# FFN of two batches at a time by seven block products, in a pooled-attention and mixture-of-depths kernel

## The chip, the cores and the metric

The kernel runs on one core of a Trainium2 chip. The metric is the device time of one execution in microseconds (us). The core has five engines that run their own instruction queues side by side: TensorE (PE in the profile, with its weight loads as PEld) for matrix products, VectorE (DVE), ScalarE (ACT), GpSimd (POOL), and SyncE (SP), which here starts the transfers between main memory and the on-chip memory (SBUF). Matrix products land in PSUM, from where ACT or DVE copy them. [...] a buffer that is used again makes its next writer wait for its last reader.

## The reference

Two stages follow each other. The first is attention with 8 batches, 8 heads, 1152 keys, 64 values per head, and queries averaged in pairs (576 rows). The second routes the 128 rows of each batch with the highest gate score through a feed-forward network (FFN) and adds the result, weighted by the gate, to those rows. All is float32.

```python
q_pool = q.reshape(B, H, S // 2, 2, D).mean(axis=3)
scores = np.matmul(q_pool, k.transpose(0, 1, 3, 2)) / np.sqrt(D)
attn = softmax(scores)                      # sum + 1e-9 in the divisor
x = np.matmul(attn, v)                      # -> (B, 576, 512), heads side by side

scores = x @ w_gate                         # (B, 576)
out = x.copy()
for b in range(B):
    top = argpartition(-scores[b], 128)[:128]
    xe = x[b, top]                          # 128 x 512
    ye = np.maximum(xe @ w1, 0) @ w2        # w1 512 x 1024, w2 1024 x 512
    g = 1 / (1 + np.exp(-scores[b, top]))
    out[b, top] = x[b, top] + g[:, None] * ye
```

## The kernel before

Two heads make a pair; 8 batches of 4 pairs are 32 pairs, and each is worked off in two halves of 288 query rows: 64 halves, numbered h. In half h, PE forms the scores of h (L818), ACT takes their exponentials into a tile p of which there are two (L825), POOL and DVE sum them, and PE forms the products of half h - 1 with v (L836). So p is used one half after it is made.

```python
def scores(self, half):
    ...
    p = half["p"] = self.work.tile([P, self.NG, G, 2, n], F32, name="p")     # work: 2 buffers
    for c in range(self.NC):                                                 # 9 blocks of keys
        sc = self.banks()                                                    # PSUM: 4 tiles of 2 banks
        for e in range(2):
            for j in range(2):
                nc.tensor.matmul(sc[keys, j, 0:n], lhsT=pair["kT"][...], rhs=pair["qT"][rows, qs], ...)  # L818
        nc.scalar.activation(p[:, c // G, c % G, :, :], sc[:, :, 0:n], AF.Exp, scale=self.scale)          # L825

def folded(self, half):                     # sums of the exponentials
    ...
    for u in range(G):
        nc.gpsimd.tensor_tensor(out=acc[:, u, :], in0=units[:, 0, u, :], in1=units[:, 1, u, :], op=ALU.add)  # L857
    for a, of in enumerate((units[:, 2, :, :], acc[:, :, :])):
        nc.vector.tensor_reduce(fold[:, a, :], of.rearrange(...), AX.X, ALU.add, apply_transpose=True)       # L862
    ...

def normalized(self, pair):
    ...
    rec = pair["rec"] = self.small.tile([P, self.QB], F32, name="rec")
    nc.vector.reciprocal(rec[:, :], tot)                                     # L954
    x = self.work.tile([P, self.QB, BLK], F32, name="x")
    nc.gpsimd.tensor_tensor(out=x, in0=pair["avb"], in1=rec (broadcast), op=ALU.mult)   # L956, shortened

def gated(self, half):
    ...
    nc.vector.tensor_reduce(pair["red"][:, ns], pair["prod"][:, ns, :], AX.X, ALU.add)
    if half["s"] == 1:
        nc.vector.tensor_tensor(out=pair["part"][:, pair["hp"], :], in0=pair["red"], in1=pair["rec"], op=ALU.mult)  # L981
        ...                                                                  # after 4 pairs: the batch is routed
```

Routing a batch is a generator (`routed`) whose pieces are laid between the pieces of the attention of later batches. It ranks the scores on DVE, finds the chosen rows (`index`, POOL, L1175), gathers them by an indirect transfer (`xe`), transposes them on PE (L1197), and then runs the FFN of that one batch:

```python
hT = ffn.tile([P, self.NFC, P], F32, name="hT")
for f0 in range(0, self.NFC, 4):                    # 8 blocks of 128 hidden units
    pv = self.banks()[:, 0, :].rearrange("p (c n) -> p c n", n=P)
    for f in range(4):
        for c in range(self.ND):                    # 4 blocks of 128 inputs
            nc.tensor.matmul(pv[:, f, 0:w], lhsT=self.w1[:, c, ...], rhs=xeT[:, c, 0:w], ...)   # L1208
        if f == 3:
            nc.scalar.activation(hT[:, f0 : f0 + 4, 0:w], pv[:, :, 0:w], AF.Relu)               # L1216
ps = self.banks()[:, 0, :]
for f in range(self.NFC):
    nc.tensor.matmul(ps[0:w, 0 : self.Dm], lhsT=hT[:, f, 0:w], rhs=self.w2[:, f, :], ...)       # L1221
...
nc.scalar.activation(y[0:w, :], ps[0:w, 0 : self.Dm], AF.Copy, scale=own_gate[0:w, 0:1])        # L1240
nc.gpsimd.tensor_tensor(out=xe[0:w, :], in0=y[0:w, :], in1=xe[0:w, :], op=ALU.add)              # L1245
nc.gpsimd.indirect_dma_start(out=rows_out, ..., in_=xe[0:w, :], ...)                            # L1246
```

Keys and queries (kb, qb) and values (v_sb) of a pair are loaded ahead: in the second half of pair n, those of pair n + 2. kb and qb have two buffers each, v_sb three. After the last half there is a tail: layer 2 of batch 5, the FFN of batch 6, and the routing and FFN of batch 7.

Of the kernel before, what the change touches and what calls it, by code (L numbers as in the profile page):

```python
# [10 lines left out]
P = 128  # L11
BLK = 32

G = 3
# [520 lines left out]
class _Plain:  # L535
# [10 lines left out]
    def __init__(self, ctx, tc, q, k, v, moe_w_gate, moe_w1, moe_w2, capacity, out):  # L546
# [27 lines left out]
        assert 0 < self.TAIL < P and self.Dm == self.ND * P and self.Dm <= 512  # L574
        assert self.F == self.NFC * P and self.NFC % 4 == 0
# [17 lines left out]
        self.w2 = self.const.tile([P, self.NFC, self.Dm], F32, name="w2")  # L593

# [21 lines left out]
    def constants(self):  # L616
# [13 lines left out]
        slot_i = self.ffn.tile([P, self.Sp], I32, name="cmp", bufs=1)  # L630
        nc.gpsimd.iota(slot_i[:, :], pattern=[[1, self.Sp]], base=0, channel_multiplier=0)
        self.slot_f = const.tile([P, self.Sp], F32, name="slot_f")
        nc.vector.tensor_copy(self.slot_f[:, :], slot_i[:, :])
# [34 lines left out]
    def line_of_scores(self):  # L668

        line = self.ffn.tile([P, self.NT * P], F32, name="sc_row")  # L670
        self.nc.gpsimd.memset(line[0:1, self.Sp :], 0.0)
        return line
# [24 lines left out]

    def load_pair(self, b, hp):  # L700
# [3 lines left out]
        qb = self.load.tile([P, self.QB, 2, BLK], F32, name="qb")  # L704
# [8 lines left out]
    def load_values(self, pair):  # L713


        nc, hp = self.nc, pair["hp"]
        v_sb = pair["v"] = self.load.tile([P, 2, self.NC, self.D], F32, name="v_sb", bufs=3)
        of = self.v[pair["b"], 2 * hp : 2 * hp + 2]
        of = of.rearrange("j (i g c) d -> g i j c d", i=BLK, c=self.NC)
        for g in range(P // BLK):  # L720
            nc.sync.dma_start(
                v_sb[g * BLK : (g + 1) * BLK, :, :, :].rearrange("i j c d -> i j (c d)"),
                of[g].rearrange("i j c d -> i j (c d)"),
            )
# [16 lines left out]
    def load_first(self, b, hp):  # L741
# [3 lines left out]
        kb = self.load.tile([P, self.KB, BLK], F32, name="kb")  # L745
        kn = kb.rearrange("p n d -> p (n d)").rearrange("p (c j d) -> p c j d", c=NC, j=2)
        acc = self.work.tile([P, G, 2 * self.HALF], F32, name="acc")
        third = self.QB // 3
        qn = acc.rearrange("p u n -> p (u n)")[0 : 3 * BLK, 0 : 4 * third * D]
        qn = qn.rearrange("p (j m d) -> p j m d", j=2, d=D)  # L750
        v_sb = self.load.tile([P, 2, NC, D], F32, name="v_sb", bufs=3)
# [11 lines left out]
        return {"k": kn, "q": qn, "v": v_sb, "b": b, "hp": hp}  # L763

    def prepare_first(self, pair):
# [5 lines left out]
        acc = self.work.tile([P, G, 2 * self.HALF], F32, name="acc")  # L771
        qp = acc.rearrange("p u n -> p (u n)")[0:rows, 0 : 2 * third * D]
        qp = qp.rearrange("p (n j d) -> p n j d", j=2, d=D)
# [76 lines left out]
    def folded(self, half):  # L850
# [9 lines left out]
        fold = self.small.tile([P, 2, G * nb], F32, name="fold")  # L860
# [8 lines left out]
        if half["s"] == 0:  # L869
            pair["sum"] = self.small.tile([P, 2, self.QB], F32, name="sum")  # L870
# [11 lines left out]
    def side_by_side(self, of):  # L882

        n = of.shape[-1]
        to = self.small.tile([BLK, P // BLK, n], F32, name="groups")
# [4 lines left out]
    def added(self, groups):  # L890
        n = groups.shape[-1]
        total = self.small.tile([BLK, n], F32, name="total")
# [26 lines left out]
    def multiplied(self, half):  # L919

        pair, hb, hp = half["pair"], self.HB, half["pair"]["hp"]
        if half["s"] == 0:
            pair["prod"] = self.work.tile([P, self.QB, BLK], F32, name="prod")
# [8 lines left out]
    def normalized(self, pair):  # L932
# [3 lines left out]
        if self.last_pair(pair):  # L936
# [16 lines left out]
        rec = pair["rec"] = self.small.tile([P, self.QB], F32, name="rec")  # L953
        nc.vector.reciprocal(rec[:, :], tot)  # L954
        x = self.work.tile([P, self.QB, BLK], F32, name="x")
        nc.gpsimd.tensor_tensor(  # L956
            out=x[:, :, :],
            in0=pair["avb"][:, :, :],
            in1=rec[:, :].unsqueeze(2).broadcast_to([P, self.QB, BLK]),
            op=ALU.mult,  # L960
        )
        pair["x"] = x
# [10 lines left out]
    def gated(self, half):  # L973

        nc, pair, hb = self.nc, half["pair"], self.HB
        if half["s"] == 0:
            pair["red"] = self.small.tile([P, self.QB], F32, name="red")
        ns = slice(half["s"] * hb, (half["s"] + 1) * hb)
        nc.vector.tensor_reduce(pair["red"][:, ns], pair["prod"][:, ns, :], AX.X, ALU.add)
        if half["s"] == 1:  # L980
            nc.vector.tensor_tensor(  # L981
# [5 lines left out]
            if pair["hp"] == self.NPAIR - 1:  # L987
                unit = self.routed(pair["b"], pair["part"])
                at = next(unit) == "mid"
                self.routing.append([pair["b"], unit, at])  # L990
# [6 lines left out]
    def routed(self, b, part):  # L997
# [8 lines left out]
        line = self.small.tile([P, self.QB], F32, name="line")  # L1006
# [4 lines left out]
        if b < self.B - 1:  # L1011
# [6 lines left out]
            else:  # L1018
                total = self.small.tile([BLK, self.QB], F32, name="total")
# [9 lines left out]
            sc_row = ffn.tile([P, NT * P], F32, name="sc_row")  # L1029
# [11 lines left out]
        else:  # L1041

            diag = ffn.tile([P, self.QB, BLK], F32, name="diag", bufs=1)
# [34 lines left out]
        for t, rows in tiles:  # L1078
            at = t * P
            cmp = ffn.tile([P, Sp], F32, name="cmp", bufs=1)  # L1080
# [20 lines left out]
            tie = ffn.tile([P, P], F32, name="tie", bufs=1)  # L1101
# [35 lines left out]
        for s0, w in self.slots:  # L1137
            pick = ffn.tile([P, NT, P], F32, name="pick", bufs=1)
            index = ffn.tile([P, 1], I32, name="index")
            own_gate = ffn.tile([P, 1], F32, name="own_gate")  # L1140
            if b == self.B - 1:
# [3 lines left out]
                    in0=self.slot_f[:, s0 : s0 + w].unsqueeze(1).broadcast_to([P, NT, w]),  # L1145
# [15 lines left out]
            else:  # L1161
# [13 lines left out]
                nc.gpsimd.tensor_scalar(  # L1175
# [6 lines left out]
            xe = ffn.tile([P, self.Dm], F32, name="xe")  # L1182
# [9 lines left out]
            yield mid  # L1192
# [8 lines left out]
            yield mid  # L1201

            hT = ffn.tile([P, self.NFC, P], F32, name="hT")
            for f0 in range(0, self.NFC, 4):
                pv = self.banks()[:, 0, :].rearrange("p (c n) -> p c n", n=P)
                for f in range(4):
                    for c in range(self.ND):
                        nc.tensor.matmul(  # L1208
                            pv[:, f, 0:w],
                            lhsT=self.w1[:, c, (f0 + f) * P : (f0 + f + 1) * P],  # L1210
                            rhs=xeT[:, c, 0:w],
                            start=(c == 0),
                            stop=(c == self.ND - 1),
                        )
                    if f == 3:
                        nc.scalar.activation(hT[:, f0 : f0 + 4, 0:w], pv[:, :, 0:w], AF.Relu)  # L1216
                    yield "hidden" if f0 + f == self.NFC - 1 else False

            ps = self.banks()[:, 0, :]
            for f in range(self.NFC):  # L1220
                nc.tensor.matmul(  # L1221
                    ps[0:w, 0 : self.Dm],
                    lhsT=hT[:, f, 0:w],
                    rhs=self.w2[:, f, :],
                    start=(f == 0),
                    stop=(f == self.NFC - 1),
                )
                yield False
            if b == self.B - 1:
                nc.vector.scalar_tensor_tensor(  # L1230
                    out=xe[0:w, :],
                    in0=ps[0:w, 0 : self.Dm],
                    scalar=own_gate[0:w, 0:1],
                    in1=xe[0:w, :],
                    op0=ALU.mult,
                    op1=ALU.add,
                )
            else:
                y = ffn.tile([P, self.Dm], F32, name="y", bufs=1)
                nc.scalar.activation(  # L1240
                    y[0:w, :], ps[0:w, 0 : self.Dm], AF.Copy, scale=own_gate[0:w, 0:1]
                )
                if b < self.B - 2:
                    yield True
# [227 lines left out]
```

## Time and profile before

Three runs: median 707.77 us (707.0 to 708.58). One profiled execution, span 704.8 us:

| engine | busy, us | share of the span |
|---|---|---|
| PE (products) | 694.4 | 99% |
| PEld (weight loads, beside PE) | 516.8 | 73% |
| DVE | 496.5 | 70% |
| POOL | 485.1 | 69% |
| ACT | 444.5 | 63% |

The 16 transfer engines moved 82.86 MB; the packets of the main queue took 58.1% of their time.

In a line of the groups, the name left of the arrow is what is written, the ones right of it what is read; then shape, type and count; after the first bar the busy time of all in us and the mean duration of one in ns; after the second bar the idle time of the engine ahead of them and who ended it. In a line of the chain the first number is the start in us, the second the length. A float32 matmul of the program shows as two records. Records of PE overlap, so a mean duration is longer than the pace at which they follow each other.

### The profile page before, as it was taken

The page shows a single profiled execution, that of the slowest core. Times are in us where ns is not written, and L with a number is a line of the kernel's source. Part 1 is how long each engine was busy: PE and PEld are TensorE (multiplying, and loading weights), DVE is VectorE, ACT ScalarE, POOL GpSimd, SP SyncE. Part 2 cuts the span into 40 slices and gives each one's busy share as a digit, 9 for nine tenths or more (in the row PEclk, how much of TensorE's full clock was granted, in tenths as well). Part 3 has the DMA queues.
Part 4 walks back from the last instruction along what each step waited for, and adds up shares of the span by engine and source line. Part 5 has one row for each costly group of instructions (what it writes and reads, how often), then busy time and mean ns, then how long its engine had stood idle before and what let it go on. Part 6 is the DMA issues. An engine that isn't in the chain of part 4 may idle for free.

```text
span 704.8 us, 23397 instructions
## 1 busy us (share of the span) xinstructions
PE 694.4 (99%) x9948; PEld 516.8 (73%) x9948; DVE 496.5 (70%) x793; ACT 444.5 (63%) x963; POOL 485.1 (69%) x452
## 2 busy tenths in 40 slices
PE   8999999999999999999999999999999999999996
PEld 5668899996758866688656887578775787766573
DVE  3877777996559965498754988559774697689540
ACT  6677778777547775477746776467754777477210
POOL 5877777868658695586955779467874877686520
PEclk9999999999999999999999999999999999999999
DMA  8888887858486483756928468382775728432200
GB/s 175 172 178 180 171 166 137 146 116 161 85 149 111 85 162 75 145 97 111 172 40 159 81 129 160 66 148 61 161 130 85 135 56 169 83 72 62 45 31 35
DMA packets 389490, 82.86 MB, mean 118 GB/s; under 512 B 376640, under 2 KB 376640, under 8 KB 389376
## 3 DMA queue, kind: packets, MB, share of 16 engines
q1 hardware_dynamic: 387872, 76.49, 58.1%
q0 software_dynamic: 1280, 4.20, 1.8%
q8 instruction: 80, 1.31, 0.8%
q10 hardware_dynamic: 224, 0.59, 0.3%
q14 instruction: 34, 0.28, 0.1%
HBM read 69.65 MB, written 11.59 MB: 115 GB/s over the span
## 4 chain that ended last, share of the span: by engine, by line
PE 89%; POOL 5%; issue 2%; DMA 1%; ACT 1%; DVE 1%; SPq 0%; POOLq 0%; DVEq 0%; ACTq 0%
PE ps L836 36%; PE ps L818 36%; PE ps L1208 8%; PE ps L1221 7%; POOL acc L857 2%; ACT p L825 1%; DMA kb<-in_k_dram 1%; DMA xe<-out_dram,index 1%; PE ps L1197 1%; POOL prod L925 1%; POOL x L956 0%; POOL av L846 0%; DVE fold L862 0%; POOL index L1175 0%; SPq L759 0%
## 5 line engine op out<-in xcount | busy, mean ns | idle before, releaser
L825 ACT ACTIVATE p<-ps 128x576 f32<-128x576 f32 x576 | 320.2, 695 | 1.7 <-PE ps L818 1.3
L818 PE MATMUL ps<-qT,kT 64*64 64x288 f32 x4608 | 295.2, 404 | 0.2 <-ACT p L825 0.2
L836 PE MATMUL ps<-p,v_sb 64*64 64x288 f32 x4608 | 294.6, 403 | 0.0
L857 POOL TENSOR_TENSOR acc<-p 128x576 f32<-128x576 f32 x192 | 266.3, 1417 | 15.4 <-ACT p L825 15.1
L836 PEld LDWEIGHTS ps<-p,v_sb 64*64 64x64 f32 x4608 | 215.5, 133 | 65.3 <-ACT p L825 9.2
L818 PEld LDWEIGHTS ps<-qT,kT 64*64 64x64 f32 x4608 | 208.0, 132 | 73.0 <-ACT p L825 15.4
L862 DVE TRANSPOSE_TENSOR_REDUCE fold<-p 128x54 f32<-128x1728 f32 x64 | 126.0, 1969 | 50.2 <-ACT p L825 50.2
L862 DVE TRANSPOSE_TENSOR_REDUCE fold<-acc 128x54 f32<-128x1728 f32 x64 | 125.3, 1957 | 46.0 <-POOL acc L857 45.8
L844 ACT COPY two<-ps 128x576 f32<-128x576 f32 x64 | 40.9, 639 | 156.9 <-PE ps L836 143.8
L846 POOL TENSOR_TENSOR av<-two 128x288 f32<-128x288 f32 x64 | 51.2, 800 | 96.5 <-ACT two L844 94.9
L915 DVE STREAM_TRANSPOSE avb<-av 128x288 f32<-128x288 f32 x64 | 29.4, 460 | 66.5 <-POOL av L846 66.5
L956 POOL TENSOR_TENSOR x<-avb,rec 128x576 f32<-128x576 f32 x32 | 37.1, 1159 | 40.3 <-DVE rec L954 27.9
L1208 PEld LDWEIGHTS ps<-xeT,w 128*128 128x128 f32 x512 | 57.8, 192 | 2.7 <-ACT p L825 2.6
L1208 PE MATMUL ps<-xeT,w 128*128 128x128 f32 x512 | 59.3, 277 | 0.0
L1221 PE MATMUL ps<-w,hT 128*128 128x512 f32 x128 | 57.3, 598 | 0.0
L925 POOL TENSOR_TENSOR prod<-avb,w_gate 128x288 f32<-128x288 f32 x64 | 51.5, 805 | 0.6 <-DVE avb L915 0.6
L902 ACT ACTIVATE sums<-total,tiny 32x18 f32<-32x18 f32 x124 | 38.1, 308 | 15.9 <-DVE total L893 14.2
L732 POOL TENSOR_TENSOR qp<-qb 128x576 f32<-128x576 f32 x31 | 43.8, 1414 | 2.2 <-DMA qb<-in_q_dram 2.2
L1221 PEld LDWEIGHTS ps<-w,hT 128*128 128x128 f32 x128 | 23.6, 190 | 28.1 <-issue 25.8
L735 DVE STREAM_TRANSPOSE kT<-kb 128x1152 f32<-128x1152 f32 x31 | 42.5, 1370 | 0.0
L887 ACT COPY groups<-sum 32x36 f32<-32x36 f32 x124 | 27.1, 219 | 6.7 <-DVE sum L872 5.2
L981 DVE TENSOR_TENSOR part<-red,rec 128x18 f32<-128x18 f32 x32 | 27.0, 845 | 1.1
(95 smaller groups left out, 290.6 us busy)
## 6 DMA issues: line engine op xcount, KB each, us to landing
kb<-in_k_dram SPq DMA_DIRECT2D x124, 144.0 KB
qb<-in_q_dram SPq DMA_DIRECT2D x124, 144.0 KB
v_sb<-in_v_dram SPq DMA_DIRECT2D x124, 144.0 KB
out_dram<-x SPq DMA_DIRECT2D x128, 72.0 KB
lines<-row_rank SPq DMA_DIRECT2D x7, 640.0 KB
w<-in_moe_w_dram SPq DMA_DIRECT2D x8, 512.0 KB
sc_row<-row SPq DMA_DIRECT2D x7, 288.0 KB
acc<-in_q_dram ACTq DMA_DIRECT2D x2, 288.0 KB
```

The source lines that it names most:

```text
L732: nc.gpsimd.tensor_tensor(out=qp[:, :, :], in0=pair["q"][:, :, 0, :], in1=pair["q"][:, :, 1, :], op=ALU.add)
L735: nc.vector.transpose(kT.rearrange("p (c g i) -> p c g i", c=self.NC, i=BLK), pair["k"].rearrange("p (g c) d -> p c g d", c=self.NC),)
L818: nc.tensor.matmul(sc[keys, j, 0:n], lhsT=pair["kT"][rows, c * P + keys.start : c * P + keys.stop], rhs=pair["qT"][rows, qs], start=True, ...
L825: nc.scalar.activation(p[:, c // G, c % G, :, :], sc[:, :, 0:n], AF.Exp, scale=self.scale)
L836: nc.tensor.matmul(av[j * self.D : (j + 1) * self.D, e, 0:n], lhsT=half["pair"]["v"][keys, j, c, :], rhs=half["p"][keys, c // G, c % G, j, :],
L844: nc.scalar.copy(two[:, :, :], av[:, :, 0:n])
L846: nc.gpsimd.tensor_tensor(out=half["av"][:, :], in0=two[:, 0, :], in1=two[:, 1, :], op=ALU.add)
L857: nc.gpsimd.tensor_tensor(out=acc[:, u, :], in0=units[:, 0, u, :], in1=units[:, 1, u, :], op=ALU.add)
L862: nc.vector.tensor_reduce(fold[:, a, :], of.rearrange("p u (m d) -> p (u m) d", d=BLK), AX.X, ALU.add, apply_transpose=True,)
L925: self.nc.gpsimd.tensor_tensor(out=pair["prod"][:, ns, :], in0=pair["avb"][:, ns, :], in1=self.w_gate[:, hp : hp + 1, :].broadcast_to([P, ...
L1208: nc.tensor.matmul(pv[:, f, 0:w], lhsT=self.w1[:, c, (f0 + f) * P : (f0 + f + 1) * P], rhs=xeT[:, c, 0:w], start=(c == 0), stop=(c == self ...
L1221: nc.tensor.matmul(ps[0:w, 0 : self.Dm], lhsT=hT[:, f, 0:w], rhs=self.w2[:, f, :], start=(f == 0), stop=(f == self.NFC - 1),)
```

## The change

Batches 0 to 5 go through the FFN two at a time. With two batches a layer is a product of 2 x 2 blocks: two batches by two halves of the inputs, times two halves of the inputs by two halves of the outputs. Eight block products would be needed; the Strassen-Winograd scheme forms them from seven, with sums of blocks ahead (s1 to s4 of the inputs, t1 to t4 of the weights) and sums of products after. Each part has its engine: t1 to t4 are formed once by VectorE, kept in main memory, and loaded in turn into one buffer `tw` of 2 MB for each layer; s1 to s4 are formed by GpSimd; the products are copied out of PSUM by ScalarE, and added up by VectorE. Batches 6 and 7 are as before.

To make room in SBUF, qb has one buffer and v_sb two, and values are loaded a half-pair closer to their use, with several small buffers shared. GpSimd's division of x moves from the half of the reciprocal to the next one (`divided`), the gather and the FFN come later by a half or more, the product of gate sums and reciprocals (`part`) goes from VectorE to GpSimd except for the last two pairs, and the index of the chosen rows from GpSimd to VectorE. The tail is ordered anew, since it now holds layer 2 of batches 4 and 5 together.

The diff, cut to its core:

```diff
+        self.paired = self.B - 2 - self.B % 2
+        self.tw = self.const.tile([P, 4, self.ND // 2 * self.F // 2], F32, name="tw")
...
+    def weight_sums(self):
+        for layer in (2, 1):
+            b11, b12, b21, b22 = (self.quarter(layer, i, j) for i in range(2) for j in range(2))
+            t1, t2, t3, t4 = (self.summed(layer, i) for i in range(4))
...
+            for i, (to, x, y) in enumerate(((t1, b12, b11), (t2, b22, t1), (t3, b22, b12), (t4, b21, t2))):
+                nc.vector.tensor_tensor(out=to, in0=x, in1=y, op=ALU.subtract)
+                nc.sync.dma_start(kept[:, i, :], self.tw[:, i, :])
+                yield
+    def load_sums(self, layer):
+        for i in range(0, 4, 2):
+            self.nc.sync.dma_start(self.tw[:, i : i + 2, :], self.tw_kept[layer][:, i : i + 2, :])
+            yield
...
-        qb = self.load.tile([P, self.QB, 2, BLK], F32, name="qb")
+        qb = self.load.tile([P, self.QB, 2, BLK], F32, name="qb", bufs=1)
...
-        v_sb = pair["v"] = self.load.tile([P, 2, self.NC, self.D], F32, name="v_sb", bufs=3)
+        v_sb = pair["v"] = self.load.tile([P, 2, self.NC, self.D], F32, name="v_sb", bufs=2)
...
+    def divided(self, pair):
+        x = pair["x"] = self.work.tile([P, self.QB, BLK], F32, name="x")
+        self.nc.gpsimd.tensor_tensor(
...
-            nc.vector.tensor_tensor(
+            ending = pair["b"] == self.B - 1 and pair["hp"] >= self.NPAIR - 2
+            engine = nc.vector if ending else nc.gpsimd
+            engine.tensor_tensor(
                 out=pair["part"][:, pair["hp"], :],
...
-                nc.gpsimd.tensor_scalar(
+                nc.vector.tensor_scalar(
                     out=index[0:w, :],
...
+    def input_sums(self, a, s):
+        for i, (to, x, y, op) in enumerate(
+            ((s1, a21, a22, add), (s2, s1, a11, subtract), (s3, a11, a21, subtract), (s4, a12, s2, subtract))
+        ):
+            self.nc.gpsimd.tensor_tensor(out=to, in0=x, in1=y, op=op)
...
+    def seven_products(self, layer, a, s, c, rest, shape):
+        steps = (
+            (a11, b11, c11, ()),
+            (s1, t1, c22, ()),
+            (s3, t3, c21, ()),
+            (s2, t2, u, ((u, c11), (c21, u), (u, c22), (c22, c21))),
+            (s4, b22, c12, ((c12, u),)),
+            (a12, b21, x, ((c11, x),)),
+            (a22, t4, y, ((c21, y),)),
+        )
+        for i, (of, by, to, _) in enumerate(steps):
+            if i % 2 == 0:
+                tile = self.banks()
...                                     # layer 1: 4 x 2 matmuls of 128 columns; layer 2: 4 of 256
+            copies.append((to, ps))
+            last = i == len(steps) - 1
+            if i % 2 or last:
+                for copy in copies:
+                    nc.scalar.copy(*copy)
+                copies = []
+            yield last
+        for *_, sums in steps:
+            for to, of in sums:
+                nc.vector.tensor_tensor(out=to, in0=to, in1=of, op=ALU.add)
...
             else:
                 loaded = None
                 if n + 2 < len(pairs):
                     loaded = self.load_pair(*pairs[n + 2])
-                    self.load_values(loaded)
+                if n + 1 < len(pairs):
+                    self.load_values(upcoming)
...
+            if h > 10 and s == 1:
+                next(sums, None)
...
+            if h > 3 and s == 0:
+                self.divided(halves[h - 3]["pair"])
```

## The prediction

> **What bounds the kernel now.** I read the busy table of the page first, then the strip of 40 slices, then who waited for whom on PE alone, then the chain that ended last in order of time, then the groups, then the timeline around one FFN and over the last 50 us.
>
> ```profile
> span 704.8 us, 23397 instructions
> ## 1 busy us (share of the span) xinstructions
> PE 694.4 (99%) x9948; PEld 516.8 (73%) x9948; DVE 496.5 (70%) x793; ACT 444.5 (63%) x963; POOL 485.1 (69%) x452
> ...
> PE   8999999999999999999999999999999999999996
> ...
> PEclk9999999999999999999999999999999999999999
> ```
>
> PE is busy from the second slice to the last, at full clock. 704.8 - 694.4 leaves 10.4 us without PE; a count of windows puts 2.2 of it before 8.79 us, 6.5 after 698.3, and 1.7 in all the rest. PE's own waits are tiny: the largest are 1.0 us at the start and 0.6 us for one gathered tile. So the time is the sum of what PE is given, and other engines matter only if they become late.
>
> What PE is given stands in the groups and, cleaner, in the chain:
>
> ```profile
> L1208 PE MATMUL ps<-xeT,w 128*128 128x128 f32 x512 | 59.3, 277 | 0.0
> L1221 PE MATMUL ps<-w,hT 128*128 128x512 f32 x128 | 57.3, 598 | 0.0
> ...
> L981 DVE TENSOR_TENSOR part<-red,rec 128x18 f32<-128x18 f32 x32 | 27.0, 845 | 1.1
> ```
> ```profile
> 171.82 4.37 PE ps L818 x72
> 176.19 7.34 PE ps L1208 x64
> 183.53 4.53 PE ps L836 x72
> 188.06 4.37 PE ps L818 x72
> 192.42 7.06 PE ps L1221 x16
> 199.49 4.53 PE ps L836 x72
> 204.01 4.37 PE ps L818 x72
> ```
>
> One float32 matmul of the program is two records here (64 records for 4 x 8 matmuls). A half of an attention pair is 4.37 + 4.37 = 8.74 us of PE; 64 halves are 559.4 us. One batch's FFN is 7.34 us for layer 1 and 7.06 for layer 2; eight are 115.2 us, the only large block of PE that the change touches. The mean of one matmul (277, 598 ns) is a latency and must not be multiplied by a count; the pace is 7.34/64 = 0.115 us for 128 columns and 0.429 us (the step between weight loads of layer 2 in the timeline) for 512. The first products after an FFN block take 4.53 instead of 4.37: entering and leaving each block costs some 0.16 us.
>
> **What the Trainium skill says.** "TensorE: Matmul & The Clock Gate", section Step-by-step: what each phase is for, says that a matmul streams one column of the moving operand per cycle and that the next weights load while the current matmul runs. The trace agrees in kind: 0.429 us for 512 columns and 0.243 us (4 x 4.37/72, four tiles of the array side by side) for 288 are 0.838 and 0.843 ns a column, and the 0.19 us weight load of layer 2 hides. "GPSIMD Engine Reference", section 8 (Key points), says that GpSimd shares its SBUF interfaces with VectorE, and that they contend when a VectorE instruction has two SBUF inputs. The trace agrees: DVE's product of 128x18 (L981) takes 845 ns, where a DVE reduction of 128x72 (L1007) takes 277. The same page, section 4.1 (Engine selection), puts GpSimd at about twice VectorE's time for two-input elementwise work; here 1.28 us on POOL (L1245, 128x512) stand against 0.76 on DVE (L1044, 128x576).
>
> **The change, part by part.**
>
> *PE, layer 1.* For a pair of batches, 2 x 64 records become 7 products x 4 blocks x 2 k-tiles x 2 records = 112, all still 128 columns: 112 x 0.1147 = 12.85 us against 14.68, so -1.83.
>
> *PE, layer 2.* 2 x 16 records of 512 columns become 7 x 4 x 2 = 56 of 256 columns. A line through 0.1128 us at 128 columns (7.22 us of weight loads over 64) and 0.429 at 512 has 0.8234 ns a column and 7 ns fixed. It gives 0.2445 at 288, where 0.243 is measured, so I trust it at 256: 0.218 us, and 56 x 0.218 = 12.2, with 0.15 for the drain 12.4. Against 14.12 that is -1.75.
>
> *PE, edges.* Six pairs of FFN blocks (layer 1 and layer 2, batches 0 to 5) become three: six entries fewer at 0.16 us, -1.0. Transposes of the gathered rows stay.
>
> *Sum on PE.* 3 x (1.83 + 1.75) + 1.0 = 11.7 us. PE's busy time should be about 682.7.
>
> *POOL.* Input sums: POOL takes 0.80 us for 288 columns and 1.28 for 512, so about 0.73 for 256. Four sums of 256 and four of 512 are 8.1 us a pair, 24.3 in all. The four adds of 256 into the gathered rows are 8.8 us against 6 x 1.28 = 7.7 before. The gate products of 30 pairs come from DVE; POOL takes 0.24 us for a five-column operation (L1118), so about 0.25 each: 7.5. The index add goes away (7 x 0.92 = 6.4). Net about +26: 512 us, still far under PE.
>
> *DVE.* Seven adds of 512 and seven of 256 a pair. By L1044 (0.76 us at 576) an add of 512 is about 0.68 and one of 256 about 0.38: 7.4 us a pair, 22 in all, and up to a few tenths more each when POOL runs beside. Eight weight sums of 1024 at about 1.25: 10. Minus 30 x 0.845 = 25 for the gate products, plus 1 for the index. Net +8: about 505 us.
>
> *ACT.* Seven copies of 512 (0.60 each), two wide Relus (1.1), seven copies of 256 (0.35) and four scalings (0.4) are 10.4 us a pair, 31 in all, against 12 x 0.59 + 6 x 0.69 = 11.2. Net +20: about 464 us.
>
> *DMA.* The weight sums are 2 MB a layer: 4 MB are stored once, and five reloads of 2 MB follow, 14 MB on top of 82.9. The share of the 16 engines was 58% on the main queue and 0.62 between 162 and 622 us.
>
> *Buffers and order.* The values of the next pair are loaded one half-pair later into two buffers instead of three, and q has one buffer instead of two. The wait for q's buffer is for POOL's pooling add, about 12 us after the start of a half of 8.74, so the load starts some 3 us into the next half; it is not needed by POOL until 16 us later. The values have about 19 us. Neither seems short. Dividing x one half later and gathering later take work off POOL where it is dense.
>
> **Where this lies on the path.** All of PE's savings lie on it. The other three engines' additions lie beside it if they fit. In the attention halves without FFN around 167 to 248 us, I count the busy times per 8.7 to 8.9 us: POOL up to 7.5, ACT up to 7.0, DVE up to 8.7. DVE is full in the halves with ranks, but has 2.65 of 8.89 and 1.67 of 8.89 in others, and exp results wait in two buffers, so one half of lateness is absorbed. The product block itself adds 12 to 13 us of PE, in which DVE and POOL have their sums to do and little else. The PSUM tiles are freed by ACT copies (1.2 us per tile of two products) faster than PE fills them (3.6 us).
>
> **The tail.** After the last attention product (658.35) PE still has 40 us of FFN. The last batch's ranking must reach PE meanwhile: its first matmul came 5.9 us after, the ranks ended 7.4 us after its columns were transposed, the gather took 4.3 us. In the new order of PE's instructions I find 6.3, 8.0 and 5.5 us of other PE work in those three places, so no new hole. The 6.5 us after PE's end, the last scaling and scatter, stay.
>
> So 707.77 - 11.7 = 696.1; I add 0.4 for small waits where sums arrive late: **696.5 us**.
>
> **The rivals.**
>
> *A VectorE or GpSimd backlog.* The seven adds are issued ahead of the folds of the same half, so the folds wait for the last product. For: DVE was at 8.71 of 8.74 in one half, and two-input DVE work suffers beside POOL. Against: the block gives DVE 12.8 us more, I put DVE's end of that half at 5 to 6 us after PE's next start instead of 3 to 4, and the folds have nearly a half of play. If it bites, a microsecond or two per block, six blocks: 698 to 705.
>
> *Transfers.* A 1 MB reload stands in front of the keys and queries on the same queue: at the 180 GB/s the strip shows at best, 5.8 us each. For: the loads are bursty (0.96 in the half from 239 us), and q now has one buffer. Against: two halves of lead before scores need them. If it bites: 699 to 706.
>
> *PE gains more.* If gaps around the gathers (0.6 us and smaller holes, 1.7 in all) close too and edges cost more than I count, 694. To pass 2% the time must go under 693.6, 14.2 us saved, which is more than all the terms I can find.
>
> *256 columns cost more than the line says.* If layer 2's weight loads, 0.19 us of a 0.218 us matmul, no longer hide well, at 0.235 us its gain shrinks by 1.0 us a pair: 699.5.
>
> **Range and chances.** The arithmetic on PE is well pinned, and what can go wrong is lateness, so the range leans upward: 693.8 to 702.5. Faster by over 2% needs a gain nowhere in the sum: 0.06. Slower by over 2% needs 26 us of new stalls against 3 us a half of slack: 0.04. Within 2%: 0.90.
>
> **What would show each step right or wrong.** PE busy near 683 at a share of 98 to 99% of a span near 693. The new product line should hold 112 x 3 records of 128 columns and 56 x 3 of 256; in the chain a layer 1 block of about 12.9 us and a layer 2 block of about 12.4. POOL near 512, DVE near 505, ACT near 464. PE's waits still under 2 us in all. I would be wrong if the chain shows pieces of DVE adds, POOL sums or loads of the weight sums between PE blocks, if the 256-column block is above 13 us, or if a hole opens after the last attention product.

## The result and the profile after

Four runs after: median 739.44 us (736.06 to 741.63), beside 708.06 (707.0 to 708.58) before. The ratio is 1.044, with a 95% interval of 1.0403 to 1.0476: the kernel became slower by 31 us, where 11 us less were expected.

The page of the changed kernel, with the lines that answer to those of before:

```profile
span 737.5 us, 23597 instructions
## 1 busy us (share of the span) xinstructions
PE 698.2 (95%) x9972; PEld 526.4 (71%) x9972; DVE 535.1 (73%) x819; ACT 465.2 (63%) x1005; POOL 525.0 (71%) x504
...
PE   8999999999999899998999999899899979989896
```

PE has holes now: 737.5 - 698.2 = 39.3 us idle against 10.4. And it is busy for 698.2 us where 682.7 were worked out. So 44 us above the expected span: 28.5 of idle time and 15.5 of work that ran at a slower pace.

The groups of the changed kernel: the product line, the adds of products, and the product of gate sums, now on POOL.

```profile
L1360 PE MATMUL ps<-tw,s 128*128 128x256 f32 x72 | 18.2, 409 | 0.6 <-POOL s L1326 0.6
...
L1373 DVE TENSOR_TENSOR hT<-hT,s 128x512 f32<-128x512 f32 (+1 forms) x15 | 12.8, 887 | 0.1
...
L1015 POOL TENSOR_TENSOR part<-red,rec 128x18 f32<-128x18 f32 x30 | 6.8, 226 | 74.9 <-DVE red L1010 73.0 <-ACT groups L916 1.9
```

All operands of line L1360 together are 336 records of 128 columns and 168 of 256, three times 112 and 56, as the count had it. The last line is the first sign of trouble: 6.8 us of work on POOL, with 74.9 us of standing still ahead of it.

The chain that ended last breaks off after four pieces here and shows nothing, so who waited for whom takes its place (total us, times, longest):

```profile
POOL part L1015 <- DVE red L1010: 73.0, 25, 6.0
...
DVE fold L891 <- POOL acc L886: 69.7, 37, 3.5
...
PE ps L847 <- ACT two L873: 19.4, 10, 3.2
ACT groups L916 <- DVE sum L901: 19.2, 9, 4.2
...
ACT hT L1400 <- DVE hT L1373: 12.0, 3, 4.8
```

PE waits at the scores (L847) for ACT's copy `two` (L873). That copy empties the PSUM tile of the attention products, and the next scores need the tile. ACT is no bottleneck, so the question is what ACT waited for: the two ACT lines name DVE's sums (L901) and DVE's adds of products (L1373). A separate hole, 6.52 us at 609.91, is at the merge of batch 6's gate sums, where PE waits for DVE's `line` (L1039).

**A hole after an FFN block.** The timeline of the changed kernel, thinned out (start, length, engine, line; in brackets the idle time before and its releaser):

```profile
639.65 4.60 PE L865 MATMUL ps<-p,v_sb 64*64 64x288 f32 x72
...
645.92 0.48 DVE L944 STREAM_TRANSPOSE avb<-av 128x288 f32<-128x288 f32 x1 [8.77 <-POOL av L875]
...
650.18 1.88 DVE L1373 TENSOR_TENSOR s<-s,hT 128x512 f32<-128x512 f32 x1
...
654.64 1.89 DVE L1373 TENSOR_TENSOR hT<-hT,s 128x512 f32<-128x512 f32 x3
655.96 1.06 ACT L1400 ACTIVATE hT<-hT 128x1024 f32<-128x1024 f32 x1 [4.76 <-DVE hT L1373]
...
656.92 0.62 ACT L873 COPY two<-ps 128x576 f32<-128x576 f32 x1
...
657.60 3.64 PE L847 MATMUL ps<-qT,kT 64*64 64x288 f32 x28 [3.12 <-ACT two L873]
```

The products of the block run from 626.94 to 639.65, where the first line begins. DVE stands idle for 8.77 us, from 637.15 to 645.92, though the first four products lie copied since 635.5 and the last since 640.4: the next thing in its queue is `avb`, which needs the attention product that PE does after the block. The adds stand behind `avb` and behind 4 us of a newer batch's ranks, and begin at 650.18. The Relu (L1400) waits for them, `two` stands behind the Relu on ACT, and the scores, begun at 652.79, stop after three tiles (24 records) for want of PSUM. Such a hole follows five of the six blocks: 2.00, 3.22, 2.00, 3.23 and 3.12 us, 13.6 together.

**What the hole does after it is over.** Windows of the same stretch of the changed kernel (window; length; PE busy and records; granted clock; DMA share; GB/s):

```profile
648.40:652.80 4.40, 4.40 (x78) 1.00 0.40 69
...
654.50:657.60 3.10, 0.00 (x1) 0.83 0.02 5
657.60:660.50 2.90, 2.90 (x24) 0.50 0.00 0
660.50:664.00 3.50, 3.50 (x40) 0.59 0.03 1
```

After the hole PE is busy but at half clock: 24 records in 2.90 us, where 4.40 us hold 78 before. Cut into windows of 3 us, the whole span has a granted clock under 0.93 at its start, behind its last product, and beside six holes (those of 1.95, 3.22, 6.52, 3.12 and 2.46 us and the first of 2.00), and nowhere else. The Trainium skill, "TensorE: Matmul & The Clock Gate", section HAM oscillation — how this bites in real kernels, tells of this: idle gaps throttle the array's clock to one half, and the next work starts slowly; it puts the limit at about 3.4 us of idleness. The trace agrees in kind and differs in size: gaps of 2.00 and 1.95 us were followed by slow blocks too (4.95 us for 48 score records that take 3.4, 6.29 for 72 that take 4.6), while others of 2.00 and 3.23 were not.

**A wait of POOL.** The timeline of the changed kernel, in a half with ranks:

```profile
155.69 0.22 POOL L1015 TENSOR_TENSOR part<-red,rec 128x18 f32<-128x18 f32 x1 [5.75 <-DVE red L1010]
155.87 4.15 POOL L886 TENSOR_TENSOR acc<-p 128x576 f32<-128x576 f32 x3
...
160.06 1.98 DVE L891 TRANSPOSE_TENSOR_REDUCE fold<-acc 128x54 f32<-128x1728 f32 x1 [2.57 <-POOL acc L886]
...
163.93 0.72 DVE L768 STREAM_TRANSPOSE qT<-qp 128x576 f32<-128x576 f32 x1
...
164.09 0.64 ACT L873 COPY two<-ps 128x576 f32<-128x576 f32 x1
...
164.81 4.59 PE L847 MATMUL ps<-qT,kT 64*64 64x288 f32 x72 [0.81 <-ACT two L873]
```

POOL stands still for 5.75 us until DVE, behind its ranks, has formed `red`. The product takes 0.22 us; but the three additions of `acc` come only after it, so DVE's own fold waits for `acc` in turn. Each engine waits for the other, and what DVE does behind the fold is late. Where the weight sums are formed besides, that reaches PE: holes of 0.81, 1.18, 0.20, 1.07, 0.83 and 1.95 us between 164 and 243 us.

It reaches PE in two ways. At 1.18 and 0.83 us the scores stop after three tiles, as behind an FFN block: DVE's `sum` is late, ACT waits 4.25 and 3.91 us for it ahead of `groups`, and `two` stands behind `groups`. At the other four the first tile of a half is late, and there the bracket misleads: it names `two` in three of them, as above, but the scores start 0.15 to 0.16 us after the end of DVE's `qT` in all four, and in the hole of 0.20, which names `qT`, ahead of `two`. PE waits for DVE's transposed queries there, and they stand behind the late fold in DVE's queue. So 3.8 of the 19.4 us that the list puts down to `two` are DVE's own.

### The profile page after: what moved, and what is told of

Same layout as the page of the kernel before. It is cut to its first block, busy times and chain, and to the rows that moved or that the text cites. A ratio compares the mean times of both kernels' runs of the same rounds, so it can differ in the third digit from the quotient of the medians.

```text
span 737.5 us, 23597 instructions
## 1 busy us (share of the span) xinstructions
PE 698.2 (95%) x9972; PEld 526.4 (71%) x9972; DVE 535.1 (73%) x819; ACT 465.2 (63%) x1005; POOL 525.0 (71%) x504
## 5 line engine op out<-in xcount | busy, mean ns | idle before, releaser
L854 ACT ACTIVATE p<-ps 128x576 f32<-128x576 f32 x576 | 321.5, 691 | 10.9 <-PE ps L847 10.6
L847 PE MATMUL ps<-qT,kT 64*64 64x288 f32 x4608 | 307.8, 416 | 19.8 <-ACT two L873 19.4
L886 POOL TENSOR_TENSOR acc<-p 128x576 f32<-128x576 f32 x192 | 278.5, 1478 | 13.3 <-ACT p L854 13.2
L847 PEld LDWEIGHTS ps<-qT,kT 64*64 64x64 f32 x4608 | 207.6, 136 | 106.5 <-ACT two L873 24.4
L891 DVE TRANSPOSE_TENSOR_REDUCE fold<-acc 128x54 f32<-128x1728 f32 x64 | 125.4, 1959 | 69.7 <-POOL acc L886 69.7
L873 ACT COPY two<-ps 128x576 f32<-128x576 f32 x64 | 40.6, 635 | 111.4 <-PE ps L865 107.5
L875 POOL TENSOR_TENSOR av<-two 128x288 f32<-128x288 f32 x64 | 53.1, 829 | 73.6 <-ACT two L873 70.4
L1015 POOL TENSOR_TENSOR part<-red,rec 128x18 f32<-128x18 f32 x30 | 6.8, 226 | 74.9 <-DVE red L1010 73.0
L931 ACT ACTIVATE sums<-total,tiny 32x18 f32<-32x18 f32 x124 | 38.2, 308 | 14.6 <-DVE total L922 12.8
L1010 DVE TENSOR_REDUCE red<-prod 128x9 f32<-128x288 f32 x64 | 27.3, 427 | 0.4 <-POOL prod L954 0.3
L1124 DVE TENSOR_SCALAR_CACHE_REDUCE pick<-sc_row,gate_sc 128x576 f32<-128x576 f32 (+4 forms) x40 | 21.6, 539 | 5.6 <-ACT gate_sc L682 5.4
L1368 ACT COPY s<-ps 128x256 f32<-128x256 f32 (+1 forms) x27 | 11.4, 446 | 21.8 <-PE ps L1360 21.8
L901 DVE TENSOR_REDUCE sum<-fold 128x18 f32<-128x108 f32 x64 | 21.8, 340 | 2.2
```

The costliest lines, as they stand in the source:

```text
L847: nc.tensor.matmul(sc[keys, j, 0:n], lhsT=pair["kT"][rows, c * P + keys.start : c * P + keys.stop], rhs=pair["qT"][rows, qs], start=True, ...
L873: nc.scalar.copy(two[:, :, :], av[:, :, 0:n])
L875: nc.gpsimd.tensor_tensor(out=half["av"][:, :], in0=two[:, 0, :], in1=two[:, 1, :], op=ALU.add)
L891: nc.vector.tensor_reduce(fold[:, a, :], of.rearrange("p u (m d) -> p (u m) d", d=BLK), AX.X, ALU.add, apply_transpose=True,)
L931: self.nc.scalar.activation(tot[rows, :], pair["total"][:, j * self.QB : (j + 1) * self.QB], AF.Identity, bias=self.tiny[0:BLK, 0:1],)
```

## The experiments

Suspects: the place of `part` on GpSimd, the place of the adds, the weight sums on VectorE, and PE's slower pace after holes. All kernels were timed beside the kernel before on the same chip; ratios are to that, with 95% intervals. Diffs are against the changed kernel unless said otherwise.

### `part` back on VectorE (e1)

```diff
-            engine = nc.vector if ending else nc.gpsimd
+            engine = nc.vector
```

> One part undone: the product of gate sums and reciprocals goes back from GpSimd to VectorE for all pairs. In the changed kernel GpSimd waited 73.0 us for VectorE ahead of this product, 25 times, with its next sums of exponentials behind it in the queue. Theory A (this wait of one engine for the other is what makes both late, and through them TensorE): the stalls before 250 us go, the late merge of batch 6 shrinks, 715 to 728 us. Theory B (the late sums of the products hold ScalarE, and with it PSUM): 736 to 744 us, since the stalls after the FFN blocks stay and VectorE gets 25 us more.

729.91 us (723.76 to 730.34), ratio 1.0294 (1.0243 to 1.0344), some 10 us better than the change. The small early holes went, and the one at the merge fell from 6.52 to 1.67, but one of 4.69 came at 185.53, which named DVE's qT; the holes after the FFN blocks stayed (2.00, 3.22, 1.99, 3.23, 3.12). So `part` is one cause and not the only one. The timeline of this kernel shows why VectorE is no good place for it either:

```profile
169.26 9.60 DVE L1015 TENSOR_TENSOR part<-red,rec 128x18 f32<-128x18 f32 x1
...
173.58 1.15 POOL L988 TENSOR_TENSOR x<-avb,rec 128x576 f32<-128x576 f32 x1
174.70 4.12 POOL L886 TENSOR_TENSOR acc<-p 128x576 f32<-128x576 f32 x3
```

A product of 128x18, 0.18 us at the least, lasted 9.60 us, until POOL's unbroken row of instructions ended at 178.82. The Trainium skill, "SBUF — State Buffer", section Who interferes with whom, says that a VectorE instruction with two SBUF inputs contends for a shared port with a GpSimd instruction that reads SBUF, and that the lock is exclusive; the trace agrees that the product is held while POOL works, and shows the wait lasting over several POOL instructions in a row. The median of this product was 0.715 us.

### The adds right behind the folds of the same half (e2)

```diff
-            yield last
+            yield "sums" if last else False
```

The place "sums" of a half stands behind its folds and ahead of the attention product; the place behind the whole half was where the adds had gone.

> One line changed: VectorE's sums of the seven products are queued right behind the folds of the same half, ahead of the transposition of the attention product that follows the FFN block, instead of behind it; instructions and sizes are the same, and so is TensorE's order. Theory B: the five stalls that follow the FFN blocks (2 to 3.2 us each, and as much again in slowed products) go, 713 to 722 us. Theory A: at most 4 us, 735 to 740 us.

720.17 us (714.78 to 721.93), ratio 1.0166 (1.0116 to 1.0217): 19 us better. All five holes behind the FFN blocks are gone; the early ones, the 6.7 us at the merge and the tail's stay. Of the 19.6 us between the two profiles, 13.6 are those holes and 7.2 are slower work of PE (698.2 against 691.0); two new holes, 0.89 at 412.92 and 0.85 at 580.96, take 1.7 back. POOL still waits 66.5 us for `red`. The groups of this kernel, by form, show the adds beside an idle POOL:

```profile
L1373 DVE TENSOR_TENSOR hT<-hT,s 128x512 f32<-128x512 f32 x12 | 7.9, 689 | 0.9 <-ACT s L1368 0.5 <-ACT hT L1368 0.2
```

0.69 us each, where the same twelve took 1.01 in the changed kernel; all 42 took 22.7 us instead of 39.4. It was the place of the adds, not the number of them.

### Without the weight sums (e3)

Leaves out the eight subtractions; blocks of the weights are stored and loaded in their place.

```diff
-                nc.vector.tensor_tensor(out=to, in0=x, in1=y, op=ALU.subtract)
-                nc.sync.dma_start(kept[:, i, :], self.tw[:, i, :])
+                nc.sync.dma_start(kept[:, i, :].rearrange(...), x)
+                if layer == 1:
+                    nc.sync.dma_start(to, x)
```

> Work left out: the eight subtractions of weight blocks on VectorE; the blocks themselves are stored and loaded in their place, so the FFN of batches 0 to 5 is computed with other numbers, at the same sizes. Theory C (the subtractions, laid into the halves between 100 and 250 us ahead of the folds, make VectorE late there): the five stalls before 250 us go, 729 to 733 us. Theories A and B: no more than 3 us, 736 to 740 us.

731.02 us (726.55 to 731.72), ratio 1.0319 (1.0279 to 1.0359). The early holes went almost whole (0.27 and 0.20 left), all others stayed. POOL still waited 66.4 us for `red` (73.0 in the changed kernel): the wait alone does not reach PE, it does so where VectorE has another 1.6 to 2.0 us in the same half.

### Without the adds (e4)

Leaves out the 42 additions of products on VectorE.

```diff
-            for to, of in sums:
-                nc.vector.tensor_tensor(out=to, in0=to, in1=of, op=ALU.add)
+            pass
```

> Work left out: all 42 sums of the seven products on VectorE, so the FFN of batches 0 to 5 is not summed up. Theory B: as with the sums queued earlier or a little lower, 708 to 720 us. Theory A: VectorE is 22 us lighter, but GpSimd still waits for it, 730 to 737 us.

718.57 us (716.9 to 721.66), ratio 1.0151 (1.0128 to 1.0173). The same as with the adds early (e2) within its spread: in the right place the adds cost next to nothing, in the wrong one some 19 us.

### The adds early, and `part` behind (f1)

On top of e2: `part` stays on GpSimd, but is queued behind the same half's `acc` and `prod`; batch 6's last one goes to VectorE, so that its `line` is formed ahead of the folds.

```diff
-            engine = nc.vector if ending else nc.gpsimd
-            engine.tensor_tensor(out=pair["part"][:, pair["hp"], :], ...)
+            left = (self.B - 1 - pair["b"]) * self.NPAIR + self.NPAIR - 1 - pair["hp"]
+            if left in (0, 1, self.NPAIR):
+                self.parted(pair, nc.vector)
+            else:
+                self.late = pair
...
                 self.multiplied(halves[h - 2])
+            if self.late:
+                self.parted(self.late, nc.gpsimd)
+                self.late = None
```

> On top of the sums queued behind the folds (720.2 us): the product of gate sums and reciprocals stays on GpSimd, but stands behind that half's sums of exponentials and gate product in its queue instead of ahead of them; batch 6's last one goes to VectorE, and its line is formed ahead of the folds, as in the kernel before. Theory A (GpSimd's wait in that place): the waits of GpSimd for VectorE fall from 66 us to under 15, the 6.7 us hole before batch 6's merge and most of the stalls before 250 us go, 704 to 711 us. If only the late merge matters and not the place in the queue: 712 to 716 us.

697.18 us (696.76 to 698.68), ratio 0.985 (0.9823 to 0.9878). Its page and its waits:

```profile
span 695.0 us, 23621 instructions
...
PE 683.1 (98%) x9972; PEld 529.8 (76%) x9972; DVE 532.3 (77%) x820; ACT 462.9 (67%) x1005; POOL 515.7 (74%) x503
```
```profile
DVE fold L891 <- POOL acc L886: 21.0, 18, 3.7
```

No instruction of `part` waits any more, the folds' wait for `acc` fell from 69.7 to 21.0 us, and only the tail's holes are left (2.38 and 0.69). VectorE has as much to do as in the changed kernel (532 against 535 us); apart from batch 6's one product nothing went from one engine to another, only the order in two queues changed.

### The weight sums in halves (f2)

On top of f1.

```diff
+                for c in range(2):
+                    at = slice(c * to.shape[1] // 2, (c + 1) * to.shape[1] // 2)
+                    nc.vector.tensor_tensor(out=to[:, at], in0=x[:, at], in1=y[:, at], op=ALU.subtract)
...
-            if h > 10 and s == 1:
+            if h > 9:
```

> On top of that, the eight subtractions of weight blocks are split in two each and laid one to a half. Theory C (the load of a whole subtraction in one half is what makes VectorE late before 250 us): what is left of the stalls there goes, 700 to 707 us. If the move of the product has already taken these stalls away: within 1.5 us of the run without the split.

695.72 us (694.5 to 698.39), ratio 0.9834 (0.9799 to 0.9868). 1.5 us from f1, inside the spread of either: with `part` behind, the long subtractions no longer hurt.

### The tail in another order (f3)

On top of f2: a piece of batches 4 and 5 moves ahead of the ranks of the last batch, and one of batch 6 from behind the gather to ahead of it.

```diff
-        pieces(older, 2)
+        pieces(older, 3)
...
-        pieces(older, 4)
-        pieces(old, self.NFC // 2 - 1)
+        pieces(older, 3)
+        pieces(old, self.NFC // 2 + 1)
...
-        pieces(old, self.NFC // 2 + 2)
+        pieces(old, self.NFC // 2 + 1)
```

> On top of that, the tail is ordered anew: one more block product ahead of the last batch's line of scores, two more pieces of batch 6 ahead of its index. The 2.4 and 0.7 us holes in the tail should close, 3 to 5 us below the run without it, so 696 to 703 us; if the holes only move, within 1.5 us.

694.27 us (692.86 to 694.41), ratio 0.9796 (0.9769 to 0.9822). The holes shrank from 2.37 and 0.69 to 0.66 and 0.49 us, and the median by 1.45, less than expected and inside the spread of f2: in f2's profile no slow pace followed these holes that could be won back. It has the lowest median of all, about 2% under the kernel before.

### Only `part` on GpSimd, in the kernel before (f4)

The diff is against the kernel before.

```diff
-            nc.vector.tensor_tensor(
+            ending = pair["b"] == self.B - 1 and pair["hp"] >= self.NPAIR - 2
+            engine = nc.vector if ending else nc.gpsimd
+            engine.tensor_tensor(
                 out=pair["part"][:, pair["hp"], :],
```

> The kernel before with one part of the change alone: the product of gate sums and reciprocals on GpSimd, ahead of that half's sums, except for the last two pairs. Theory A in its strong form (this wait alone makes the engines late): 710 to 720 us, with stalls of TensorE ahead of scores. Weak form (it costs GpSimd and VectorE their slack, which the kernel before has and the changed one needs): 706 to 710 us, with over 40 us of GpSimd waiting for VectorE and no stall of TensorE.

728.45 us (727.59 to 736.11), ratio 1.0287 (1.0259 to 1.0315). This one line makes the kernel before 20 us slower, more than expected, and by another way. Its waits:

```profile
DVE fold L862 <- POOL acc L857: 75.3, 43, 3.6
...
POOL x L956 <- DVE rec L954: 40.8, 17, 4.2
PE ps L1199 <- DMA xe<-out_dram,index: 18.0, 7, 3.2
```

The profiled execution is the slowest of its five (736.11). Here `part` itself waits little (10.6 us), while POOL waits for DVE at x (40.8 us, 27.9 before). But DVE's folds wait for POOL's `acc`, and DVE forms the place of the chosen rows (`pick`) later: at one gather, POOL's index stands 1.0 us behind the start of PE's half, where it stood 0.9 ahead of the start in the kernel before. So the gather is late, and PE waits for its rows, seven times. In the change the gather comes later, and that wait is absent. So f4 shows that this order is harmful in both kernels, not that its cost in the change is 20 us by the same wait.

### `part` behind, without the early adds (g1)

The diff is against f1.

```diff
-            yield "sums" if last else False
+            yield last
```

> The changed kernel with the product of gate sums and reciprocals behind that half's sums in GpSimd's queue, and batch 6's line early, but the sums of the seven products as late as they were: the fourth corner of the square whose others are 739.4 (neither), 720.2 (sums early), 697.2 (both). If the two causes add up: 739.4 - 23.0 = 716 us, with the five stalls after FFN blocks left and those before 250 us gone. If they feed each other (a late engine makes the other wait longer): off that by more than 4 us.

719.58 us (718.64 to 721.49), ratio 1.0187 (1.0166 to 1.0209). The mirror of e2: the early holes are gone and the five behind the FFN blocks are back (2.00, 3.23, 2.00, 3.23, 3.12). With the changed kernel, e2 and f1 it completes a square: 739.4, 720.2 (adds early), 719.6 (`part` behind), 697.2 (both). If the two simply added up, both would give 720.2 + 719.6 - 739.4 = 700.4; 3 us from what was measured; 1.7 of them are the two new holes of e2, which f1 does not have. They are two faults, nearly independent, of 19 and 20 us.

### Only `line` early, `part` still ahead (g2)

On top of e2: only batch 6's last product goes to VectorE; all others go to GpSimd ahead of `acc`, as in the change.

```diff
+            if left in (0, 1, self.NPAIR):
+                self.parted(pair, nc.vector)
+            else:
+                self.parted(pair, nc.gpsimd, True)
```

> The sums of the seven products early, the product of gate sums and reciprocals ahead of that half's sums as in the change, and only batch 6's line early and on VectorE. If the place in GpSimd's queue is what counts: 710 to 715 us, the stalls before 250 us and GpSimd's 66 us of waiting stay. If the late merge of batch 6 was nearly all: 699 to 705 us.

717.88 us (715.58 to 718.38), ratio 1.016 (1.0143 to 1.0177). Only 2 us better than e2. The early holes stayed, and the hole at the merge (6.90 us) too: its `part` on VectorE lasted 6.76 us beside POOL, where the same product took 0.97 in f1. So it is the place of the other `part`s in POOL's queue, and with it of the `line` of batches 0 to 5, that brought f1's other 21 us, the hole at the merge included.

### `part` on VectorE in the late place (g3)

The diff is against f3.

```diff
-                self.parted(self.late, nc.gpsimd)
+                self.parted(self.late, nc.vector)
```

> The best kernel so far (694.3 us) with that product on VectorE in all pairs, in the same late place. In an earlier run one such product of 128x18 took 9.6 us on VectorE, as long as GpSimd ran without a pause. If this starving matters for the path: 698 to 706 us, with products of several us. If the slack takes it up: within 2 us of 694.3.

696.68 us (694.96 to 704.86), ratio 0.9885 (0.9815 to 0.9955). Between 0.17 and 5.81 us for one product, median 0.55, and yet only about 2 us slower than f3 in the median, with PE holes of 0.50 and 1.65 us. Its runs scatter too much for more.

### Planted holes in the kernel before (g4)

Against the kernel before: in every eighth half PE must wait for a tiny transfer that starts when `two` is there.

```diff
+                if h < n_halves and h % 8 == 5:
+                    gap = self.small.tile([P, 4], F32, name="gap", bufs=1)
+                    nc.scalar.dma_start(gap[:, :], done["two"][:, 0, 0:4])
+                    ps = self.banks()[:, 0, 0:4]
+                    nc.tensor.matmul(ps, lhsT=self.ident[:, :], rhs=gap[:, :], start=True, stop=True)
```

> The kernel before with eight planted waits of TensorE, one in every eighth half: a product of 4 columns that reads what a small transfer brings after the half's attention product has been copied out; an estimated 3 us each. Nothing else is changed. If a gap costs itself: 8 x 3 = 24 us, 728 to 736 us, and attention products keep their pace of 4.37 us. If TensorE is also slower after a gap (theory D): up to as much again, 737 to 758 us, with a granted clock near 0.5 after some of the gaps.

740.49 us (737.36 to 744.78), ratio 1.0463 (1.0436 to 1.049). Eight holes of 2.55 to 2.59 us, 20.5 us in all, made the kernel 34 us slower. Two of the eight in its timeline:

```profile
320.58 0.36 PE L1372 MATMUL ps<-gap,ident 128*128 128x4 f32 x2 [2.55 <-DMA gap<-two]
320.87 4.60 PE L818 MATMUL ps<-qT,kT 64*64 64x288 f32 x72
...
410.50 0.36 PE L1372 MATMUL ps<-gap,ident 128*128 128x4 f32 x2 [2.56 <-DMA gap<-two]
410.78 6.28 PE L818 MATMUL ps<-qT,kT 64*64 64x288 f32 x72
```

In the profiled run, 38 us longer than the profiled one of before (743.0 against 704.8), of eight equal holes three were followed by a slow block (7.55, 6.28 and 6.28 us) and five by one of 4.6. Those three are 6.3 us more; the planted matmuls' own records take 3.1; two waits for gathered rows (4.24 and 1.16) and the slow block behind the longer one (6.88) are nearly all the rest. So a hole can cost more than its length, some 0.8 us on average here, but not each time: beyond their own length these eight cost nothing (five), 1.7 us (two) or 3.0 us (one). In the change the share was larger, 15.1 us of slower work (698.2 against 683.1 in f1) on some 29 us of holes.

## Why the prediction was wrong, point by point

**PE's sum was right.** A block of layer 1 took 12.70 us (12.85 said), one of layer 2 12.28 (12.4), so the rival of dearer products of 256 columns is out. Where the holes are gone, PE is busy for 680.5 (f2) to 683.1 us (f1), where 682.7 stood, and f2's 695.72 us is 0.8 from the predicted 696.5. The arithmetic saves what it was said to save; the change's order of queues loses 43 us again.

**ACT and DMA were right, POOL nearly.** ACT 465.2 us against 464; POOL 525.0 against 512 (515.7 in f1). No PE wait names a load of the weight sums, so the second rival played no part.

**VectorE's sum was mis-sized, without weight.** 535.1 us against 505. The adds took 39.4 (22 said), the weight sums 14.6 (10 said), since the "few tenths more each when POOL runs beside" were left out of the sum: in the early place of e2, mostly beside an idle POOL, the adds took 22.7. But f1 has 532.3 us and is fast.

**What failed is the part on the path: "All of PE's savings lie on it. The other three engines' additions lie beside it if they fit."** They fitted by amount and not by order, in three places.

1. *The first rival* said that "the seven adds are issued ahead of the folds of the same half", that "the block gives DVE 12.8 us more", and that it would bite by a microsecond or two per block. The right engine, but the adds' place was misread: they stand at the end of the half, behind `avb`, which waits for PE itself. The adds could use none of the 12.8 us (DVE stood idle for 8.77 us around the block's end), and the Relu took `two`, and with it PSUM, along. e2 and e4 show it: 19 to 21 us.

2. *POOL's term*, "The gate products of 30 pairs come from DVE", was booked as 7.5 us more for POOL and 25 less for DVE. The 6.8 us of busy time are right; what was left out is the wait it brings into an in-order queue ahead of `acc`: 73.0 us of POOL. "Exp results wait in two buffers, so one half of lateness is absorbed" did not help, since the lateness takes another way: through DVE's folds to `qT`, for which PE itself waits, and through ACT's queue to `two` and PSUM. g1, g2 and f1 show it: 20 us, the hole at the merge of batch 6 included.

3. *The tail*: "no new hole". The last batch's ranks reached PE 8.6 us after the last attention product (681.0 to 689.58), and not 5.9; the other work laid there, 6.1 us of it, left a hole of 2.46, and 0.69 followed behind the gather. The traces show what the 5.9 left out: the last two `part` products, still on DVE, took 2.84 and 1.75 us the first beside input sums that are new on POOL, the second beside two divisions of x in a row; in the kernel before they took 0.92 and 0.62, 3.0 us less. That POOL is the cause was not tested here. f3 took 2 us of these holes away by laying more of PE's work there.

**And a cost that no step had:** a hole can make PE slow after it. Some 15 of the 43 us are slower work of PE (698.2 against 683.1 in f1), contained in the 19 and 20 us of points 1 and 2 (7.2 and 7.9).

How point 2 splits can be read from the profiles of e2 and f1, 717.9 and 695.0 us long: 6.1 us of early holes, 1.7 of two later ones, 6.8 at the merge, and 7.9 of slower work (691.0 against 683.1).

What stays open: why one hole is followed by half clock and another of the same length isn't.

## What to carry to other kernels

When work moves to an engine with time to spare, look at what stands behind it in that engine's queue and at what it must wait for: 0.23 us of work can hold up 4 us of another's input. A long block on PE is a gift to the others only if their work for it is queued inside it, ahead of whatever waits for PE. Follow a PSUM tile to the instruction that frees it, and read everything that stands ahead of that one on its engine. Where a view names an engine for a wait, check against the times whether the named instruction can be what the waiter needs.

## What was unexpected of the hardware

- A two-input VectorE product of 128x18 took from 0.18 to 9.60 us in e1, the longest beside a row of POOL instructions without a pause (at most 5.81 in g3 and 6.76 in g2).
- PE fell to half clock after holes as short as 1.95 to 2.6 us, for about 3 us of work or more, but after only three of eight planted holes of 2.55 to 2.59 us.
